# Sliding-window value products: a 64-column stationary side for the oldest key block

## The chip, the cores and the metric

The kernel runs on one core of a Trainium2 chip. The metric is device time in microseconds of one execution, the median of three runs. A core has TensorE (PE; its weight loads are listed as PEld), VectorE (DVE), ScalarE (ACT), GpSimd (POOL) and SyncE (SP), which here issues most DMAs. A matmul holds its stationary side (the weights, up to 128 rows by 128 columns) in the array and streams the moving side through it; the number of stationary columns is the number of partitions that it writes in PSUM.

## The reference

The model has four layers on x of 1 x 2048 x 512 in bf16, A, B, A, B, each with a residual: `x = x + layer(layernorm(x))`. Both have 32 heads of 16. A is linear attention. B, the part that matters here, is causal attention in a window of 256 keys:

```python
scores = jnp.einsum("bhqd,bhkd->bhqk", q, k) * (Dh ** -0.5)
mask = (idx[:, None] - idx[None, :] >= 0) & (idx[:, None] - idx[None, :] < W)   # W = 256
p = _softmax(jnp.where(mask[None, None], scores, -1e9), axis=-1)
o = jnp.einsum("bhqk,bhkd->bhqd", p, v)
```

## The kernel before

The 2048 tokens are 16 tiles (j) of 128. A `Plan` records every operation with what it reads and writes; `place` (L92) then gives each its engine, its place in the order and its PSUM bank from a table stored in the file (L872), and `synchronise` (L135) works out the semaphore waits. `play` (L988) sends each engine its operations in that order. So the order on every engine is fixed, and one operation can hold many instructions.

Two heads are worked on together: their keys (64 of each head) are interleaved to the 128 partitions of a key block b, so a tile of 128 tokens has two key blocks, 2j and 2j + 1. Sixteen such pairs of heads are numbered r = 4f + gq. For a layer B:

- `b_scores` (L634 to 670): scores of key block b of tile j against the queries that see it, matmuls of 32 rows by 128 columns (L650), four side by side in the array; then the exponential on ScalarE into the buffer pb (L660), and the causal mask on VectorE (L668).
- `b_far` (L672 to 725): the far 64 queries of a key block (L690, and in the last layer L693, with 32 x 64 tiles), the exponential (L703) and the mask of the window's end (L713 for a part, L721 and L722).
- The probabilities of a block lie as 320 columns of a row of 704: 384(b mod 2) + 0 to 320, and the 64 columns from 320 to 384 between the two blocks are zero. They are cleared once at the start (L364, "c24") and for a fourth buffer at L818 ("zero").
- `b_values` (L727 to 757): for each tile j, half h and f, one operation of 4 x (number of blocks) matmuls (L742). Each takes 128 columns of probabilities of one block as the stationary side and 34 columns of the values vB (2 heads x 16, and a column of ones for each head, for the sum) as the moving side, and adds to 34 columns of a PSUM bank. With j >= 2 a tile has six blocks, at the column offsets c = 0, -64, 64, 128, 192 and 256. At c = -64 the first 64 columns read are the zero pad, and at c = 256 the last 64 are. VectorE divides by the sums (L753, L754).
- `b_out` (L759): the transpose of the output, the product with wo (L412) and the residual (L585).

`feat` (L417 to 429) has 128-column matmuls for queries and keys (L426), `tok` (L404 to 415) 512-column ones (L412). The denominators of layer A (L554) use tiles of 128 rows by 32 columns. Layer B's work of a tile is interleaved with the projections of later tiles and the next layer's keys.

Of the kernel before, what the change touches and what calls it, by code (L numbers as in the profile page):

```python
# [11 lines left out]
P = 128  # L12
# [179 lines left out]
def dve(n, kind="psum"):  # L192

    if kind == "psum":
        return 65 + 1.04 * n, 148 + 1.04 * n
    if kind == "2x":
        return 68 + 0.52 * n, 151 + 0.52 * n
    if kind == "ptr":
        return 60 + 0.52 * n, 145 + 0.52 * n
    if kind == "4x":  # L200
        return 68 + 0.26 * n, 151 + 0.26 * n
    if kind == "recip":
        return 65 + 6.4 * n, 148 + 6.4 * n
    if kind == "bf":
        return 65 + 0.52 * n, 148 + 0.52 * n
    raise KeyError(kind)
# [23 lines left out]
class Plan:  # L230
# [496 lines left out]
    def b_values(self, j, h, key):  # L727
        K = self
        rp = self.rp
        ps = Tile(1, K.cls)  # L730
        blocks = [(2 * j, 0), (2 * j + 1, -64), (2 * j - 1, 64), (2 * j - 2, 128), (2 * j - 3, 192), (2 * j - 4, 256)]
        blocks = [(b, c) for b, c in blocks if b >= 0]
        reads = []
        for f in (2 * h, 2 * h + 1):
            def put(e, f=f):
                m = None
                for gq in range(4):
                    r = 4 * f + gq
                    u = 4 * (f - 2 * h) + gq
                    for i, (b, c) in enumerate(blocks):  # L740
                        o = 384 * (b % 2) + c
                        m = e.matmul(K.ps(ps)[:, 34 * u:34 * u + 34], K.P((b // 2) % rp)[:, f, gq % 2 * 2 + gq // 2, o:o + P], K.vB[:, (b // 2) % 4, b % 2, r, :], start=i == 0, stop=i == len(blocks) - 1)  # L742
                return m
            rd = []
            for i in range(max(0, j - 2), j + 1):
                rd += [("P", i % K.rp, f)] + [("vB", i % 4, a, b) for a in range(2) for b in range(2)]
                rd += [("P", i % K.rp, f, b, h_) for h_ in range(3) for b in (0, 1)]
            if j >= 2:
                rd += [("F", (j - 2) % K.rp, h_) for h_ in (0, 1)] + [("F", (j - 2) % K.rp, h_, 1) for h_ in (0, 1)]
            self.pe("pv", put, key - 0.001 * (f % 2), 4 * len(blocks), 34, rd=rd, ps=[ps])  # L750
        s = j % 2
        v = lambda: K.ps(ps)[:, 0:272].rearrange("p (u a d) -> p u a d", u=8, a=2)
        self.on("DVE", "rcp", lambda e: e.reciprocal(K.rc[:, s, h, :].rearrange("p (u a) -> p u a", a=2), v()[:, :, :, 16]), key + 0.02, dve(16, "recip"), wr=[("rc", s, h)], ps=[ps])  # L753
        self.on("DVE", "div", lambda e: e.tensor_tensor(  # L754
            K.o[:, s, :].rearrange("p (a r d) -> p r a d", a=2, d=DH)[:, 8 * h:8 * h + 8],
            v()[:, :, :, 0:16], K.rc[:, s, h, :].rearrange("p (u a) -> p u a", a=2).unsqueeze(3).to_broadcast([P, 8, 2, DH]), ALU.mult),
            key + 0.03, dve(256), rd=[("rc", s, h)], wr=[("o", s, h)], ps=[ps])
# [327 lines left out]
```

## Time and profile before

| | |
|---|---|
| median of 3 runs | 411.4 us (410.81 to 411.58) |
| the profiled execution | 410.39 us |
| its span | 408.7 us |
| granted TensorE clock | 1.00 |
| instructions | 18140, of which 7997 matmuls and as many weight loads in the page's count |

In the rows below a matmul group reads "line, engine, operation, output<-inputs, rows*columns of the stationary side, output shape, count | busy us, mean ns of one | idle time before it and what ended it". In the timeline the first two columns are start and length of a row of like instructions, in us from the start of the span. A matmul's length includes its way through the array, so like matmuls overlap, and their rate is read from their starts. In the rows of one line the three numbers are min, median and max of one instruction's length in ns.

### The profile page before, as it was taken

The numbers are of one execution on the slowest core, as the hardware profiler recorded it, in microseconds if no ns is written. First come the engines' busy times: TensorE is split into PE (matmuls) and PEld (weight loads), VectorE is DVE, ScalarE is ACT, GpSimd is POOL, SyncE is SP. The second block draws the span as 40 slices with busy tenths as digits, with TensorE's granted clock in tenths as the row PEclk, the third lists the DMA queues.
The fourth block names the chain that finished last, engine by engine and source line by source line (L and its number), as shares of the span: only waits on it lengthen the run. The fifth ranks groups of instructions, "written<-read, shape, count | busy, mean of one in ns | idle before, by whom it ended". The sixth has DMA issues, their size and how long they took to land.

```text
span 408.7 us, 18140 instructions
## 1 busy us (share of the span) xinstructions
PE 396.5 (97%) x7997; PEld 262.5 (64%) x7997; DVE 343.9 (84%) x819; ACT 355.7 (87%) x466; POOL 115.7 (28%) x185
## 2 busy tenths in 40 slices
PE   8999999999999999999999999999999999999996
PEld 3654776766575576565566777676756766566664
DVE  7985899899999898997778879988898867876675
ACT  2998769999999999999998265999999899999992
POOL 5746422113342231521322102111213123432132
PEclk9999999999999999999999999999999999999999
DMA  7794025833342443344143100345224542352463
GB/s 246 189 197 80 2 62 146 126 92 83 67 108 43 126 101 82 93 101 101 42 68 60 25 2 28 80 107 109 55 76 103 133 69 60 104 120 79 102 135 105
DMA packets 67750, 37.88 MB, mean 93 GB/s; under 512 B 48248, under 2 KB 62840, under 8 KB 67672
## 3 DMA queue, kind: packets, MB, share of 16 engines
q1 hardware_dynamic: 67328, 35.80, 38.1%
q8 instruction: 63, 1.03, 1.1%
q0 software_dynamic: 336, 0.92, 0.6%
q14 instruction: 15, 0.12, 0.1%
q10 hardware_dynamic: 8, 0.00, 0.0%
HBM read 6.29 MB, written 2.10 MB: 21 GB/s over the span
## 4 chain that ended last, share of the span: by engine, by line
PE 66%; ACT 22%; DVE 7%; DMA 2%; issue 1%; POOL 0%; SPq 0%
PE ps L412 23%; PE ps L426 16%; ACT pb L660 14%; PE ps L742 11%; PE ps L650 6%; PE ps L492 3%; ACT pb L703 3%; ACT vp L660 2%; DMA xT<-xn 2%; PE ps L693 2%; ACT tE L435 1%; PE ps L690 1%; ACT vp L703 1%; PE ps L468 1%; DVE XQ L574 1%
## 5 line engine op out<-in xcount | busy, mean ns | idle before, releaser
L660 ACT ACTIVATE pb<-ps 128x1024 bf16<-128x1024 f32 (+3 forms) x224 | 197.8, 977 | 8.3 <-PE ps L650 7.3
L742 PEld LDWEIGHTS ps<-vB,pb 128*128 128x128 bf16 x2560 | 77.9, 96 | 11.3 <-issue 3.6
L742 PE MATMUL ps<-vB,pb 128*128 128x34 bf16 x2560 | 83.7, 177 | 0.8 <-issue 0.5
L426 PE MATMUL ps<-xT,wBp 128*128 128x128 bf16 x1024 | 70.2, 219 | 0.6 <-DMA xT<-xn 0.6
L426 PEld LDWEIGHTS ps<-xT,wBp 128*128 128x128 bf16 x1024 | 58.6, 98 | 12.3 <-issue 4.2
L721 POOL TENSOR_SCALAR_AFFINE_SELECT pb<-pb 128x1024 bf16<-128x1024 bf16 x35 | 40.7, 1162 | 67.9 <-DVE pb L713 28.8
L375 POOL TENSOR_SCALAR ve<-mv 128x1 f32<-128x1 f32 x38 | 9.7, 254 | 158.3 <-DVE mv L374 157.7
L435 ACT ACTIVATE tE<-ps 128x512 bf16<-128x512 f32 x64 | 38.1, 608 | 16.6 <-PE ps L412 9.1
L703 ACT ACTIVATE pb<-ps 128x1024 bf16<-128x1024 f32 x50 | 49.2, 1053 | 2.3 <-PE ps L693 1.3
L650 PE MATMUL ps<-XQ,kB 32*128 32x256 bf16 (+2 forms) x1024 | 48.0, 262 | 2.6 <-DVE vp L603 0.6
L412 PE MATMUL ps<-wA,XQ 128*128 128x512 bf16 x192 | 49.4, 379 | 0.2 <-DVE XQ L574 0.2
L585 DVE TENSOR_TENSOR xres<-ps,xres 128x512 bf16<-128x512 f32 x63 | 42.9, 683 | 7.9 <-PE ps L412 7.6
L376 POOL TENSOR_TENSOR rs<-ve,negh 128x1 f32<-128x1 f32 x64 | 38.6, 604 | 36.1 <-DVE ve L375 31.7
L373 DVE BATCH_NORM_STATS2 stats<-xres 128x6 f32<-128x512 bf16 x64 | 43.6, 683 | 2.4 <-DMA xres<-in_A_x_dram 1.7
L426 PE MATMUL ps<-XQ,wA 128*128 128x128 bf16 x512 | 35.1, 219 | 0.1
L412 PE MATMUL ps<-wBv,xT 128*128 128x512 bf16 x128 | 35.0, 381 | 0.0
L650 PEld LDWEIGHTS ps<-XQ,kB 32*128 32x128 bf16 x1024 | 15.3, 92 | 30.7 <-ACT pb L660 9.5
L426 PEld LDWEIGHTS ps<-XQ,wA 128*128 128x128 bf16 x512 | 30.4, 98 | 5.7 <-issue 0.6
L412 PE MATMUL ps<-M,XQ 128*128 128x512 bf16 x128 | 33.7, 380 | 0.1
L412 PE MATMUL ps<-wBo,oT 128*128 128x512 bf16 x124 | 33.2, 381 | 0.3 <-ACT pb L660 0.3
L668 DVE TENSOR_TENSOR pb<-pb,tri 128x512 bf16<-128x512 bf16 x68 | 28.1, 417 | 3.8 <-ACT pb L660 3.4
L412 PEld LDWEIGHTS ps<-wA,XQ 128*128 128x128 bf16 x192 | 16.6, 97 | 18.1 <-issue 1.0
(120 smaller groups left out, 566.8 us busy)
## 6 DMA issues: line engine op xcount, KB each, us to landing
vB<-vS SPq DMA_DIRECT2D x64, 136.0 KB, 2.6
kB<-vp SPq DMA_DIRECT2D x64, 128.0 KB, 2.2
wA<-in_A_wqkv_dram SPq DMA_DIRECT2D x3, 512.0 KB, 5.2
xres<-in_A_x_dram SPq DMA_DIRECT2D x2, 512.0 KB
pb<-in_B_wqkv_dram SPq DMA_DIRECT2D x1, 1024.0 KB, 5.5
out_dram<-xres SPq DMA_DIRECT2D x8, 128.0 KB, 3.2
out_dram<-xres POOLq DMA_DIRECT2D x7, 128.0 KB, 2.8
xres<-in_A_x_dram SPq DMA_DIRECT2D x3, 256.0 KB, 3.2
```

The costliest lines, as they stand in the source:

```text
L373: self.on("DVE", "stats", lambda e: e.bn_stats(K.stats[:, t, :], K.xres[:, t, :]), key, dve(512), rd=[("xres", t)], wr=[("stats", t)])
L376: self.pow = self.on("POOL", "pow", lambda e: e.tensor_tensor(K.rs[:, t, :], K.ve[:, t, :], K.negh[:], ALU.pow), key + 0.03, (640, 690), r ...
L412: m = e.matmul(K.ps(ps), lhs(c), rhs(c), start=c == 0, stop=c == 3)
L426: m = e.matmul(K.ps(ps)[:, f * P:(f + 1) * P], w(c, f), xT(c), start=c == 0, stop=c == 3)
L435: self.on("ACT", "E", lambda e: e.activation(K.tE[:, s, :], K.ps(ps), ACT.Exp, bias=0.0), key, act(512), wr=[("tE", s)], ps=[ps])
L585: self.on("DVE", "res", lambda e: e.tensor_tensor(K.xres[:, t, :], K.ps(po), K.xres[:, t, :], ALU.add), key, dve(512), rd=[("xres", t)], w ...
L650: m = e.matmul(K.ps(two(gq // 2)[gq % 2])[:, ns * i:ns * i + ns], K.kB[rows, j % 4, 2 * f + b, :, :], K.XQ[rows, f, q:q + ns], start=True, ...
L660: return e.activation(out(h, ns).rearrange("p (f g) c -> p f g c", f=n), i, ACT.Exp, bias=0.0, scale=0.25)
L668: return e.tensor_tensor(x, x, K.tri[:, 0, :].unsqueeze(1).to_broadcast([P, 4 * n, 64]), ALU.mult)
L703: return e.activation(o.rearrange("p (f g) b c -> p f g b c", g=2), i, ACT.Exp, bias=0.0, scale=0.25)
L721: return e.affine_select(out=x, in_=x, compare_op=ALU.is_ge, fill=0.0, base=-2, pattern=[[0, 16], [-2, 64]], channel_multiplier=1)
L742: m = e.matmul(K.ps(ps)[:, 34 * u:34 * u + 34], K.P((b // 2) % rp)[:, f, gq % 2 * 2 + gq // 2, o:o + P], K.vB[:, (b // 2) % 4, b % 2, r, : ...
```

## The change

For tiles with j >= 2, the last two of the six blocks change places, so that the oldest block (2j - 4, at c = 256) is fifth and the one at c = 192 is last and closes the sum. The matmul of the oldest block takes 64 columns of probabilities, and writes 64 partitions, in place of 128: the 64 columns that are left out are the zero pad. Memory, masks, waits and the table of orders are as they were.

```diff
         blocks = [(b, c) for b, c in blocks if b >= 0]
+        if j >= 2:
+            blocks[-2:] = blocks[:-3:-1]
...
                         o = 384 * (b % 2) + c
-                        m = e.matmul(K.ps(ps)[:, 34 * u:34 * u + 34], K.P((b // 2) % rp)[:, f, gq % 2 * 2 + gq // 2, o:o + P], K.vB[:, (b // 2) % 4, b % 2, r, :], start=i == 0, stop=i == len(blocks) - 1)
+                        w = 64 if c == 256 else P
+                        m = e.matmul(K.ps(ps)[0:w, 34 * u:34 * u + 34], K.P((b // 2) % rp)[:, f, gq % 2 * 2 + gq // 2, o:o + w], K.vB[:, (b // 2) % 4, b % 2, r, :], start=i == 0, stop=i == len(blocks) - 1)
```

## The prediction

> **What bounds the kernel now.** I read the page first: busy time, the slices with the granted clock, then the costliest groups. After that come the busy times of the two stretches that hold all value products, and last the timeline of TensorE alone, because a busy PE in this profile is a modelled figure and has to be checked against start times.
>
> ```profile
> PE 396.5 (97%) x7997; PEld 262.5 (64%) x7997; DVE 343.9 (84%) x819; ACT 355.7 (87%) x466; POOL 115.7 (28%) x185
> ...
> PE   8999999999999999999999999999999999999996
> ...
> PEclk9999999999999999999999999999999999999999
> ...
> PE 66%; ACT 22%; DVE 7%; DMA 2%; issue 1%; POOL 0%; SPq 0%
> ...
> L742 PE MATMUL ps<-vB,pb 128*128 128x34 bf16 x2560 | 83.7, 177 | 0.8 <-issue 0.5
> ```
> ```profile
> sum 282.00, PE 272.06 PEld 182.09 DVE 235.12 ACT 264.53 POOL 75.19; mean PE 136.03 PEld 91.05 DVE 117.56 ACT 132.27 POOL 37.60
> ```
>
> The second fence is the sum over 76 to 220 us and 270 to 408 us. TensorE is idle there for 282.00 - 272.06 = 9.9 us and ScalarE for 282.00 - 264.53 = 17.5 us. The two are nearly balanced, with TensorE the fuller one and its clock never cut. The chain of waits gives 22% to ScalarE, but while the chain runs through ScalarE, TensorE has other work queued; what ScalarE really costs TensorE is inside those 9.9 us.
>
> The timeline around one value group of 48 products (start, length):
>
> ```profile
> 149.69 0.38 PE L412 MATMUL ps<-M,XQ 128*128 128x512 bf16 x1
> ...
> 150.00 0.40 PE L650 MATMUL ps<-XQ,kB 32*128 32x256 bf16 x8
> ...
> 150.33 1.37 PE L742 MATMUL ps<-vB,pb 128*128 128x34 bf16 x48
> ...
> 151.63 0.40 PE L650 MATMUL ps<-XQ,kB 32*128 32x256 bf16 x8
> ...
> 151.96 1.04 PE L412 MATMUL ps<-wBv,xT 128*128 128x512 bf16 x4
> ```
>
> A length runs to the end of the last matmul of the row. One product has a mean of 177 ns, so the 48 starts cover 1.37 - 0.177 = 1.19 us, 47 steps of 25 ns. The next row starts as soon as the previous ones let it: TensorE is issuing all the time. So whatever is added to the value products is added to the kernel, less what of the 9.9 us idle can be filled.
>
> **What the change does to the instruction stream.** In the built program 448 of the 2,880 value products (14 query tiles with j >= 2, 16 groups each, 2 layers) have a tile of 128 rows by 64 columns. All others keep 128x128. Each narrow product is fifth of six, so it has wide ones on both sides, inside its own group and in the next. No instruction goes away: the memsets of the zero pad stay (the block at c = -64 still reads the pad), as do the masks, the copies, the DMAs and every wait. On the four other engines the order is unchanged, and nothing moves past a queue. So the whole effect is this: 448 products with another shape, and 896 changes of TensorE's tile shape, two per narrow product.
>
> **Cost of a change of shape.** The trace has no 128x64 matmul, so I take the nearest rows, the denominators, which change only the columns (128x128 to 128x32 and back):
>
> ```profile
> 240.32 0.61 PE L426 MATMUL ps<-XQ,wA 128*128 128x128 bf16 x8
> 240.85 0.24 PE L554 MATMUL ps<-ones,eps 128*32 128x128 bf16 x4
> 240.92 0.40 PE L554 MATMUL ps<-XQ,zs 128*32 128x128 bf16 x16
> 241.25 0.62 PE L426 MATMUL ps<-XQ,wA 128*128 128x128 bf16 x8
> ```
> ```profile
> L426 PE MATMUL ps<-XQ,wA 128*128 128x128 bf16 x512 | 35.1, 219 | 0.1
> L554 PE MATMUL ps<-XQ,zs 128*32 128x128 bf16 x128 | 3.2, 219 | 0.0
> ```
>
> The last of the 8 wide ones starts at 240.32 + 0.61 - 0.219 = 240.71 us, the first 128x32 one at 240.85: 0.14 us instead of the usual step of (0.61 - 0.219)/7 = 56 ns. Back again: last start 240.92 + 0.40 - 0.219 = 241.10, next 241.25: 0.15 us. Each direction costs about 0.09 us above the step. The change of rows in the fence before gives the same: the last of 48 starts at 150.33 + 1.37 - 0.177 = 151.52, the next shape at 151.63, 0.11 us for a step that is 25 ns otherwise. I take 108 ns from a wide product to a narrow one, 83 more than 25.
>
> **Cost of the narrow load.** Two views show how long a matmul waits for its own weights, by its duration (min/median/max):
>
> ```profile
> L693 PE MATMUL ps<-XQ,kB x896: 184/209/213, 260.3 to 384.5; 32*64 32x64 bf16 x180
> ```
> ```profile
> L690 PE MATMUL ps<-XQ,kB x448: 188/188/198, 85.5 to 217.0; 32*128 32x64 bf16 x150
> ```
> ```profile
> L742 PE MATMUL ps<-vB,pb x2560: 177/177/191, 74.5 to 402.9; 128*128 128x34 bf16 x197
> ```
>
> L693 and L690 both move 64 columns; with a 64-column weight side a matmul lasts 209 ns, with 128 columns 188: 21 ns of waiting. The 191 of the third row belongs to the first product after a change of shape:
>
> ```profile
> 150.33 0.19 PE L742 MATMUL ps<-vB,pb 128*128 128x34 bf16 x1
> ```
>
> It lasts 191 - 177 = 14 ns longer, so the step to the second product is 25 + 14 = 39 ns. After a narrow product the way back is the moving time of 34 columns (56 ns for 128, so 14), the change (0.15 us - 0.056 = 94) and the wait for its weights (21): 129 ns.
>
> [...]
>
> **The sum.** Six starts of a group today: 6 x 25 = 150 ns. Afterwards: 39 + 3 x 25 + 108 + 129 = 351 ns. That is 201 ns per narrow product and 448 x 201 = 90.0 us on TensorE. Of this the idle time takes some: ScalarE and VectorE get that much more time for unchanged work, so most waits of TensorE for them shrink. I take 7 of the 9.9 us (the tiles j = 0 and 1 and the tail have waits that stay) and no new wait: TensorE's order is fixed, and ScalarE, for which score tiles are queued, only gets later input. 90.0 - 7 = 83 us. The profiled execution took 410.39 us (span 408.7 and 1.7 around it), giving 493.4; the median of the runs is 411.4, 1.0 above it, so **494.4 us**.
>
> Bounds: from below, both changes at 83 and no waits for loads, 448 x 166 = 74.4 us, with all 9.9 us filled: +64.5, 476 us. From above, the narrow load costs twice the 21 ns seen (128 rows are loaded, the row has 32): 222 x 448 = 99.5 us, nothing filled, and 3 us of new waits: +102.5, 514 us.
>
> **Rivals.**
> - *Only one of the two changes drains the array* (say narrow to wide is free, since the narrow tile is a corner of the wide array). Then a group costs about 150 + 83 + 14, 448 x 97 = 43.5 us less 7: 448 us. Against it: both directions of the denominators' rows cost the same.
> - *ScalarE sets the pace and hides part.* Its busy share in the stretches is 94%. If the 9.9 us of idle time were not the limit and half of the 90 us went behind it, the time is 456 us. Against it: the timeline shows TensorE without gaps, and ScalarE's idle 17.5 us would have to be time that TensorE could use.
> - *No drain at all*, because a 128x64 tile at the origin is no new shape to the array. Then the price is the load alone, 0 to 21 ns: up to +9.4 us, 411 to 421 us. No row excludes it, since no row has 128x64. [...]
> - *Faster.* No drain, and the 25 ns step is set by the weight load, so that half the columns take half the step: 12.5 x 448 = 5.6 us off, 406 us. It decides only if the cost of a change is under 6 ns, half the saving, against 94 in the rows. [...]
> - *The change does not do what it says*: it does, the shapes stand in the built program.
>
> **How the numbers follow.** Forecast (both changes drain, little hidden) 0.85; one drain 0.04; hidden behind ScalarE 0.03; no drain 0.06, of which a third each for slower, within 0.2% and faster; faster by a shorter load 0.02. The range is 474 to 514 us: the bounds of the forecast's case, which holds over 8 in 10 alone. A measurement tells about 0.2% from no change. Slower by over 0.2%: 0.85 + 0.04 + 0.03 + 0.02 = 0.94; within 0.02; faster 0.02 + 0.02 = 0.04.
>
> **What would show it.** A value group of 48 should last about 8 x 0.351 + 0.14 = 2.95 us instead of 1.37, the narrow ones standing alone between wide ones with about 0.11 and 0.13 us to their neighbours. ScalarE's share should fall to 355.7 / 492 = 72% and VectorE's to 70%, their busy times unchanged; TensorE's waits for ScalarE should shrink. The forecast is wrong if the narrow products start 25 ns after their neighbours (no drain), if only one side shows a gap, or if the groups grow as said and the span does not (then ScalarE, by a wait of TensorE for it, has the rest).

## The result, and the profile after

The changed kernel takes 547.27 us (543.86 to 549.96, four runs) against 411.16 us: 1.3305 times the time before, 95% interval 1.3225 to 1.3386. The forecast was 494.4 us, and its range ended at 514. The direction and the first mechanism were right; 53 us were missing from the sum.

The page of the changed kernel, the lines that answer to those of before (busy times, slices, clock, the chain that ended last, the value products' loads and products):

```profile
span 542.1 us, 18066 instructions
PE 523.5 (97%) x7923; PEld 350.3 (65%) x7997; DVE 343.3 (63%) x819; ACT 360.9 (67%) x466; POOL 114.9 (21%) x185
...
PE   8999999999999999999999999999999999999997
...
PEclk9999999997889879997899999987679866767566
...
PE 87%; DVE 5%; ACT 4%; issue 2%; DVEq 0%
...
L660 ACT ACTIVATE pb<-ps 128x1024 bf16<-128x1024 f32 (+3 forms) x224 | 200.6, 959 | 100.6 <-PE ps L650 100.4
L745 PE MATMUL ps<-vB,pb 128*128 128x34 bf16 (+1 forms) x2560 | 177.5, 188 | 0.3 <-DVE XQ L401 0.2
```

TensorE is the only bound left: the chain went from 66% to 87% TensorE, and ScalarE, with about the same work (360.9 us busy, before 355.7), now sits idle 100 us waiting for scores. The surprise is the line PEclk. It was 9 in all 40 slices; now it is under 9 in 20 of them, and the mean granted clock is 0.865.

The price of a change of tile shape is there as forecast ("drain" below: the stretch in which no product starts while the shape changes). One value group, weight loads of TensorE in four short windows that follow each other (start, length):

```profile
166.26 0.17 PEld L745 LDWEIGHTS ps<-vB,pb 128*128 128x128 bf16 x4
```
```profile
166.46 0.11 PEld L745 LDWEIGHTS ps<-vB,pb 128*64 128x64 bf16 x1
```
```profile
166.60 0.19 PEld L745 LDWEIGHTS ps<-vB,pb 128*128 128x128 bf16 x5
```
```profile
166.82 0.11 PEld L745 LDWEIGHTS ps<-vB,pb 128*64 128x64 bf16 x1
```

Loads that follow each other every 25 ns stop for the narrow one, which stands alone, and start again after it. From one narrow load to the next, 166.82 - 166.46 = 0.36 us, where six products took 150 ns. Products in a later stretch at full clock, where the rows of four begin with the narrow one and the rows of two are the wide pair before the next (start, length):

```profile
498.63 0.38 PE L745 MATMUL ps<-vB,pb 128*64 128x34 bf16 x4
498.85 0.20 PE L745 MATMUL ps<-vB,vp 128*128 128x34 bf16 x2
498.98 0.38 PE L745 MATMUL ps<-vB,pb 128*64 128x34 bf16 x4
499.21 0.20 PE L745 MATMUL ps<-vB,vp 128*128 128x34 bf16 x2
499.34 0.38 PE L745 MATMUL ps<-vB,pb 128*64 128x34 bf16 x4
```

The narrow one stands 0.13 us after the first of that pair, so 0.11 after the second. The next pair starts 0.22 to 0.23 us after the narrow one, and the steps of the three wide ones between take 39 + 25 + 25 ns of it, which leaves 0.13 to 0.14 for the way back. Read start by start, the two changes are 107 and 136 ns. A whole group of 48 at full clock takes 3.02 us (forecast 2.95, before 1.37):

```profile
166.27 3.02 PE L745 MATMUL ps<-vB,pb 128*128 128x34 bf16 x48
```

And this is how the clock goes. Busy times of the changed kernel in four windows of 3.41 us (PE, PEld, DVE, ACT, POOL, then the granted clock), and the timeline of TensorE there:

```profile
143.37:146.78 3.41, 3.41 (x15) 0.97 (x14) 2.02 (x5) 2.41 (x3) 0.00 (x0) 0.50 0.19 38
146.78:150.19 3.41, 3.41 (x64) 2.56 (x56) 1.88 (x6) 1.94 (x2) 0.00 (x0) 1.00 0.38 94
150.19:153.60 3.41, 3.08 (x31) 1.45 (x28) 2.39 (x7) 2.85 (x3) 0.00 (x0) 0.50 0.50 108
153.60:157.02 3.41, 3.41 (x86) 2.97 (x83) 1.36 (x5) 1.87 (x3) 0.79 (x2) 1.00 0.02 5
```
```profile
143.74 1.91 PE L412 MATMUL ps<-wA,XQ 128*128 128x512 bf16 x4
...
146.91 3.03 PE L745 MATMUL ps<-vB,pb 128*128 128x34 bf16 x48
149.87 0.40 PE L650 MATMUL ps<-XQ,kB 32*128 32x256 bf16 x8
150.60 1.49 PE L412 MATMUL ps<-wBo,oT 128*128 128x512 bf16 x3 [0.33 <-issue]
```

The clock is either whole or half, for one window or several. The window that begins at 146.78 holds a value group of 48 and little else; the next one, from 150.19, runs at half clock. In such a window TensorE has work, its products are only slow: three 512-column ones at 150.60 last 1.49 us and four at 143.74, in the half-clock window before, 1.91 us, both 0.44 us apart, where they are 0.22 apart at full clock. (The 0.33 us before 150.60 belong to a fourth one, whose record is missing; its weight load is there.) In this trace the clock has no other values than 0.50 and 1.00, and from one change of it to the next it is 3.41 us or a multiple of that (the longest stretch between two changes, at 1.00, lasts 88.75 us, 26 times 3.413).

What decides can be counted from the records. For each such window I added up the columns that its matmuls moved. A matmul in a 32-row strip counts as a quarter: four of 256 columns last 0.29 us in the trace of before, where one lasts 0.28 (L650). One on a 128 x 32 tile too: the 16 of 128 columns at 240.92 us there last 0.40 us together and one 0.22, so their starts lie within 0.18 us, where 16 steps of 56 ns would be 0.90. One on a 32 x 64 tile counts as an eighth, by its share of the area of a 128 x 128 one, which is my estimate; the trace of before shows 64 of 64 columns in 0.70 us, 8 ns from start to start (L693, at 260.33 us). The narrow products count whole. In these profiles 74 to 76 matmul records are missing, all of 512-column products, and they are counted by their weight loads, which are there. At full clock the 512-column products start every 216 ns and the 128-column ones every 56, so 384 columns take 160 ns, 2.4 a nanosecond, and a window has room for 8,192. The window from 146.78 has 48 x 34 = 1,632 and one group of scores, 8 x 256 / 4 = 512: 2,144, or 26%. Over the six profiles in which the clock changes often enough to find the windows (this one, and those of five experiments below):

| columns moved in the window | full-clock windows | followed by half clock | half-clock windows | followed by full clock |
|---|---|---|---|---|
| under 2,800 | 37 | 37 | 36 | 0 |
| 2,800 to 3,200 | 28 | 11 | 17 | 6 |
| over 3,200 | 687 | 0 | 41 | 41 |

The limit lies near 3,000 columns per window in both directions. That is 37% of what the array can move at full clock, but 73% at half clock, so a window that has once been lost is hard to win back: the low clock keeps itself low.

### The profile page after: what moved, and what is told of

It reads as the page before. It is cut to its first block, busy times and chain, and to the rows that moved or that the text cites. A ratio compares the mean times of both kernels' runs of the same rounds, so it can differ in the third digit from the quotient of the medians.

```text
span 542.1 us, 18066 instructions
## 1 busy us (share of the span) xinstructions
PE 523.5 (97%) x7923; PEld 350.3 (65%) x7997; DVE 343.3 (63%) x819; ACT 360.9 (67%) x466; POOL 114.9 (21%) x185
## 4 chain that ended last, share of the span: by engine, by line
PE 87%; DVE 5%; ACT 4%; issue 2%; DVEq 0%
PE ps L745 33%; PE ps L412 23%; PE ps L426 15%; PE ps L650 7%; PE ps L492 3%; ACT pb L660 2%; PE ps L693 2%; PE ps L1001 1%; PE ps L468 1%; DVE XQ L574 1%; PE ps L690 1%; ACT tE L435 1%; DVE xres L585 1%; ACT pb L703 1%; PE ps L274 1%
## 5 line engine op out<-in xcount | busy, mean ns | idle before, releaser
L660 ACT ACTIVATE pb<-ps 128x1024 bf16<-128x1024 f32 (+3 forms) x224 | 200.6, 959 | 100.6 <-PE ps L650 100.4
L745 PE MATMUL ps<-vB,pb 128*128 128x34 bf16 (+1 forms) x2560 | 177.5, 188 | 0.3 <-DVE XQ L401 0.2
L745 PEld LDWEIGHTS ps<-vB,pb 128*128 128x128 bf16 (+1 forms) x2560 | 140.6, 101 | 38.4 <-issue 5.8
L756 DVE RECIPROCAL rc<-ps 128x16 f32<-128x16 f32 x64 | 16.4, 257 | 106.8 <-PE ps L745 106.6
L426 PE MATMUL ps<-xT,wBp 128*128 128x128 bf16 x1024 | 79.8, 236 | 0.0
L426 PEld LDWEIGHTS ps<-xT,wBp 128*128 128x128 bf16 x1024 | 67.3, 106 | 12.8 <-issue 6.2
L650 PE MATMUL ps<-XQ,kB 32*128 32x256 bf16 (+2 forms) x1024 | 53.9, 290 | 1.5 <-ACT vp L703 0.5
L412 PE MATMUL ps<-wA,XQ 128*128 128x512 bf16 x176 | 50.7, 410 | 2.3 <-issue 0.9
L376 POOL TENSOR_TENSOR rs<-ve,negh 128x1 f32<-128x1 f32 x64 | 38.1, 596 | 45.7 <-DVE ve L375 41.6
L745 PE MATMUL ps<-vB,vp 128*128 128x34 bf16 (+1 forms) x320 | 41.5, 196 | 0.0
L412 PE MATMUL ps<-wBo,oT 128*128 128x512 bf16 x104 | 35.7, 453 | 3.4 <-issue 2.0
L650 PEld LDWEIGHTS ps<-XQ,kB 32*128 32x128 bf16 x1024 | 15.8, 95 | 35.5 <-ACT pb L660 10.1
```

The lines of the kernel that those rows point to most:

```text
L376: self.pow = self.on("POOL", "pow", lambda e: e.tensor_tensor(K.rs[:, t, :], K.ve[:, t, :], K.negh[:], ALU.pow), key + 0.03, (640, 690), r ...
L412: m = e.matmul(K.ps(ps), lhs(c), rhs(c), start=c == 0, stop=c == 3)
L426: m = e.matmul(K.ps(ps)[:, f * P:(f + 1) * P], w(c, f), xT(c), start=c == 0, stop=c == 3)
L650: m = e.matmul(K.ps(two(gq // 2)[gq % 2])[:, ns * i:ns * i + ns], K.kB[rows, j % 4, 2 * f + b, :, :], K.XQ[rows, f, q:q + ns], start=True, ...
L660: return e.activation(out(h, ns).rearrange("p (f g) c -> p f g c", f=n), i, ACT.Exp, bias=0.0, scale=0.25)
L745: m = e.matmul(K.ps(ps)[0:w, 34 * u:34 * u + 34], K.P((b // 2) % rp)[:, f, gq % 2 * 2 + gq // 2, o:o + w], K.vB[:, (b // 2) % 4, b % 2, r, ...
```

## The experiments

**Theory:** two prices. Each change of TensorE's tile shape drains the array (wide to narrow 107 ns from start to start, back 136, and 39 to the second wide product in place of 25 each), and the value products then move so few columns per microsecond that the clock is halved. **Rivals:** the price is on any stationary side under 128 columns; the price is on each narrow product; the shape changes themselves halve the clock.

**The order alone.** Blocks exchanged, all products 128 wide:

```diff
-                        w = 64 if c == 256 else P
+                        w = P
```

> Only the exchange of the last two blocks, all products 128 columns wide. Both theories: 411 us, a value group of 48 in 1.37 us, clock 1.00. If the order had a price of its own, it would show here.

Measured: 412.62 us, ratio 1.0012 (0.9978 to 1.0047), span 408.8 us. The exchange of the blocks costs nothing that can be measured.

**72 columns.** The same with 72 columns, narrower than 128 but wider than 64:

```diff
-                        w = 64 if c == 256 else P
+                        w = 72 if c == 256 else P
```

> The oldest block has 72 columns in place of 64, so the tile stays 128x128 and no shape changes. Theory (the change of tile shape costs, 208 ns per narrow product at full clock in the trace of the changed kernel): no drain, only a slower load of 0 to 35 ns for 448 products, 411 to 427 us, clock 1.00. Rival (any stationary side under 128 columns costs the gap): about 25 + 200 ns per product and the clock falls as in the changed kernel, 540 us.

Measured: 414.9 us, ratio 1.0046 (1.0021 to 1.0071), span 413.1 us, clock 0.999. Its line PEclk, and the groups of the value products by shape (busy, mean ns of one):

```profile
PEclk9999999999999999999999999999999999999999
...
L745 PE MATMUL ps<-vB,pb 128*128 128x34 bf16 x2160 | 88.2, 177 | 0.9 <-issue 0.6 <-DVE XQ L401 0.2
L745 PEld LDWEIGHTS ps<-vB,pb 128*128 128x128 bf16 x2160 | 82.0, 97 | 11.3 <-issue 4.1 <-ACT pb L660 2.0 <-DVE pb L668 0.8
L745 PE MATMUL ps<-vB,pb 128*72 128x34 bf16 x400 | 65.8, 187 | 0.4 <-issue 0.4
L745 PEld LDWEIGHTS ps<-vB,pb 128*72 128x72 bf16 x400 | 44.0, 110 | 0.5 <-issue 0.5
```

A 72-column load lasts 110 ns, one of 128 columns 97, and its product takes 10 ns longer (187 against 177). 448 x 10 = 4.5 us, of which the time shows 1.6 (414.9 less 413.35, the kernel before on the same chip). So eight columns more leave 2 us of the 136 that the changed kernel lost. A group of 48 takes 1.45 us (before 1.37, the changed kernel 3.02), so a side under 128 columns is not what costs: 64 columns have the two gaps, 72 have none. That the array takes 64 columns as another tile shape and 72 as the whole one is my reading of this; the rows give sizes alone. Fewer columns are no saving either, the narrower load is the slower one. (The 35 ns that the expectation allows for a load was an estimate that no run shows; measured are 13 ns more in the load and 10 in the product.)

**Side by side.** In an operation, 20 wide products first, then its four narrow ones:

```diff
-                    for i, (b, c) in enumerate(blocks):
+                todo = [(gq, i) for gq in range(4) for i in range(len(blocks)) if blocks[i][1] != 256]
+                todo += [(gq, i) for gq in range(4) for i in range(len(blocks)) if blocks[i][1] == 256]
+                for n, (gq, i) in enumerate(todo):
...
```

(The marks for the start and the stop of a sum then stand at the first and the last product of the operation.)

> The four 64-column products of an operation stand side by side behind its 20 wide ones: 224 shape changes in place of 896, the same 448 narrow products. Theory (price per change): an operation costs 14 + 82 + 112 = about 208 ns for its two changes and up to 35 ns for each narrow load, 112 operations, 23 to 39 us more on TensorE, 425 to 450 us, clock near 1.00. Rival (price per narrow product): as the changed kernel, 540 us.

Measured: 429.73 us, ratio 1.0396 (1.035 to 1.0442), span 427.7 us, clock 0.996. All 448 narrow products are there, with a quarter of the changes, and 19.0 us of the 133.4 by which the span had grown are left. Priced per change it is 112 x 208 ns = 23 us, with 4 hidden (or 7, by the 16.4 us between the medians, 429.73 and the 413.35 of the kernel before on the same chip). The price is on the change, not on the narrow product:

```profile
L747 PE MATMUL ps<-vB,pb 128*64 128x34 bf16 x400 | 30.0, 189 | 0.0
```

against 84.7 us busy for the same 400 in the changed kernel:

```profile
L745 PE MATMUL ps<-vB,pb 128*64 128x34 bf16 x400 | 84.7, 212 | 0.0
```

**One moving column.** The kernel before, with as much time added but no shape change:

```diff
+                        for _ in range(8 if i == 4 and len(blocks) == 6 else 0):
+                            e.matmul(K.ps(ps)[:, 300:301], K.P((b // 2) % rp)[:, f, gq % 2 * 2 + gq // 2, o:o + P], K.vB[:, (b // 2) % 4, b % 2, r, 0:1], start=False, stop=False, skip_group_check=True)
```

> The kernel before, all products 128 wide in the old order, with 8 more 128-column products of one moving column for each group of six (they write PSUM columns that nobody reads): 8 x 25 = 200 ns more per group, about what the two shape changes add, and no shape change; 448 groups, 90 us on TensorE. In a group 6 x 34 + 8 columns move in 350 ns, as little as in the changed kernel. Theory (the clock is halved in windows in which little moves through the array): the clock falls to 0.85 to 0.90 and the time is 530 to 550 us. Rival (the shape changes, or the gaps without a matmul that they make, halve the clock): the clock stays 1.00 and the time is 490 to 500 us.

Measured: 540.3 us (four runs, 535.52 to 546.94), ratio 1.3041 (1.2957 to 1.3126). The profile is that of the longest, span 545.2 us, clock 0.871; the other three have 0.871 to 0.886. Its page:

```profile
PE 520.4 (95%) x11505; PEld 373.9 (69%) x11581; DVE 344.2 (63%) x819; ACT 361.5 (66%) x466; POOL 114.9 (21%) x185
...
PEclk9999999997868878997899999979687769877676
```

Nearly the same line PEclk as that of the changed kernel, with no shape change added and products every 25 ns. So neither the drain nor a gap is needed to lose the clock (0.871 here, 0.865 in the changed kernel): few columns moving through the array are enough.

**A quarter and a half of the narrow products:**

```diff
-                        w = 64 if c == 256 else P
+                        w = 64 if c == 256 and gq < 1 else P      # and gq < 2
```

> Narrow products for one of the four gq of an operation: 112 narrow ones, 224 shape changes, one per operation of 24. Price per change: 112 x 208 ns = 23 us, less what is hidden, 425 to 434 us, about the same as with four narrow ones side by side, which has the same number of changes. Activity theory: a value group of 48 moves 48 x 34 columns in 1.6 us, the rest of a clock window of 3.4 us is dense, so the clock stays over 0.98. Rival (each change throttles): a quarter of the loss of the changed kernel, clock about 0.965, 435 to 450 us.

Measured: 432.56 us, ratio 1.0488 (1.043 to 1.0546), span 431.6 us, clock 0.991.

> Narrow products for two of the four gq: 224 narrow ones, 448 shape changes. Changes: 224 x 208 ns = 47 us, less some 8 hidden. Activity theory: a value group of 48 takes 2.2 us; a window of 3.4 us with one group in it stands near half activity, so the clock falls in part of the windows, less than proportionally: 0.95 to 0.99, 450 to 470 us. Rival (each change throttles): half of the loss, clock 0.93, 475 to 480 us.

Measured: 462.6 us, ratio 1.1207 (1.1141 to 1.1272), span 457.7 us, clock 0.977. Spans over that of before (408.7): 112 narrow products 22.9 us, 224 49.0, 448 133.4. The first two are 204 and 219 ns each, near the price of the two changes; the last is 298. The loss is not proportional, as a limit on the clock would have it. (By the medians, each against that of the kernel before that was run beside it, the three are 19.9, 49.9 and 136.1 us, or 177, 223 and 304 ns each.) The quarter also has as many changes as the version side by side, with a quarter of the narrow products, and costs about as much (22.9 against 19.0 us): again the change is what counts.

**Fillers.** The changed kernel, with one or three wide products of 238 moving columns more in each group of six:

```diff
+                        for _ in range(1 if i == 1 and len(blocks) == 6 else 0):      # and range(3 ...)
+                            e.matmul(K.ps(ps)[:, 272:510].rearrange("p (u d) -> p u d", d=34), K.P((b // 2) % rp)[:, f, gq % 2 * 2 + gq // 2, o:o + P], K.vB[:, (b // 2) % 4, b % 2, 0:7, :], start=False, stop=False, skip_group_check=True)
```

> The changed kernel, and in each group of six one more 128-column product with 238 moving columns (into PSUM columns that nobody reads), 102 ns each, 46 us for 448. In a group 6 x 34 + 238 = 442 columns move in 460 ns, 40% of the array's cycles against 24%. Activity theory with the limit near half: the clock is still cut but less, 0.88 to 0.95, 560 to 590 us. Rival (each change throttles): 896 changes as before, the same lost time as in the changed kernel, 547 + 46 = 593 us at a clock of 0.87.

Measured: 551.18 us, ratio 1.3361 (1.3284 to 1.3438), span 546.5 us, clock 0.994. This is outside both expectations, and on the theory's side: 46 us of work more than in the changed kernel, and 4 us more time. The clock came back almost whole at 40% of the columns, so the limit that I had put near half is lower; the table above has it at 37%.

```profile
PE 527.5 (97%) x8371; PEld 372.7 (68%) x8445; DVE 344.0 (63%) x819; ACT 360.1 (66%) x466; POOL 114.7 (21%) x185
...
PEclk9999999999999999999999999999998999899999
```

> The changed kernel, and in each group of six three such products, 137 us for 448. 918 columns move in 664 ns, 58% of the array's cycles, as much as in the value groups before the change (34 columns in 25 ns, 57%). Activity theory: the clock is back at 1.00 in spite of the 896 shape changes, and the time is 411 + 93 (the changes) + 137 less some 8 hidden, 625 to 640 us. Rival (each change throttles): the clock loss stays, 547 + 137 = 684 us at 0.89.

Measured: 637.03 us, ratio 1.5451 (1.5365 to 1.5537), span 635.4 us, clock 1.000, with all 896 changes. Its line PEclk, and from the timeline the bare price of a group (the three fillers, then the products to the next ones):

```profile
PEclk9999999999999999999999999999999999999999
...
189.94 0.46 PE L747 MATMUL ps<-vB,pb 128*128 128x238 bf16 x3
190.24 0.51 PE L745 MATMUL ps<-vB,pb 128*128 128x34 bf16 x6
190.60 0.47 PE L747 MATMUL ps<-vB,pb 128*128 128x238 bf16 x3
190.91 0.51 PE L745 MATMUL ps<-vB,pb 128*128 128x34 bf16 x6
191.27 0.47 PE L747 MATMUL ps<-vB,pb 128*128 128x238 bf16 x3
```

From filler to filler 0.66 to 0.67 us; less three times 102 ns (238 columns at 2.4 a nanosecond, and the 2.7 ns that the 512-column step of 216 ns has beyond its 213.3) leaves 0.357 us for six products, 207 ns more than 150. Spans: 448 x 207 ns = 92.7 us and 448 x 306 = 137.1 make 229.8; measured 635.4 - 408.7 = 226.7. By the medians on one chip the difference is 637.03 - 412.71 = 224.3. With one filler, 92.7 + 45.7 = 138.4; measured 137.8, in which the windows that its clock of 0.994 still lost are contained. So the sum closes to 3 to 6 us once the clock is whole.

## Why the prediction was wrong

- **What bounds the kernel: right.** It is TensorE, issuing without gaps. The added time went through, and ScalarE's share fell to 67%, where 72% was named for a shorter span.
- **The instruction stream, 448 products and 896 changes: right.** The exchange of the blocks costs nothing.
- **Cost of a change, from the columns-only rows of the denominators: right.** Forecast 108 ns in, 129 out, 39 to the next, 351 a group; measured 107, 136, 39 and 357. The way out is 7 ns longer. 90.0 us forecast, 92.7 measured. The one-drain and no-drain rivals and the faster one fall with it.
- **Cost of the narrow load: near.** It stood in the sum as 21 ns of waiting where a wide one has 14, 7 more. Measured are 7 ns more than forecast on the way out, and 7 per step where narrow ones follow each other (32 ns for 25).
- **Hidden time: not settled.** 7 us were taken off. The runs with a whole or nearly whole clock show 3 to 7 (three fillers 3 by the spans and 5.5 by the medians on one chip, side by side 4 and 7). The kernel before itself took 409.96 to 415.81 us in the runs beside the experiments, with clocks of 0.991 to 1.000, so 3 and 7 can't be told apart.
- **The sum: the step that failed.** It multiplied steps measured at clock 1.00 and never asked whether the clock would stay there. "Its clock never cut" was read as a property of the kernel; it was a result of how many columns the value groups move, 34 in 25 ns, 57% of the array, and the change took that to 204 columns in 357 ns, 24%, for 3 us at a time, nearly a whole window. Without it the span would be 408.7 + 92.7 less 3 to 7, about 494 to 498 us and a time of 496 to 500, inside the range. With it the span is 542.1: 44 to 48 us are the clock. The mean clock of 0.865 means 0.135 x 542.1 / 0.5 = 146 us at half clock. That they cost some 46 and not 73 fits with what stretches there: the steps of the 512-column products double (0.44 us for 0.22), but drains and loads stretch little. From 501.8 to 518.8 us, at half clock, the loads of the value products last 104 to 109 ns for 128 columns and 128 for 64; from 495.0 to 501.7, at full clock, 96 and 106. In a stretch at half clock the narrow products (the rows that begin with one) stand 0.42 us apart, where they are 0.36 apart at full clock:

```profile
506.87 0.38 PE L745 MATMUL ps<-vB,vp 128*64 128x34 bf16 x2
507.08 0.28 PE L745 MATMUL ps<-vB,pb 128*128 128x34 bf16 x4
507.29 0.38 PE L745 MATMUL ps<-vB,vp 128*64 128x34 bf16 x2
507.50 0.28 PE L745 MATMUL ps<-vB,pb 128*128 128x34 bf16 x4
507.71 0.38 PE L745 MATMUL ps<-vB,vp 128*64 128x34 bf16 x2
```

- **Rivals:** five were named, none of them a lower clock. A rival of the form "so few columns move that the clock is cut" could have been named from before's own rows, by the columns per microsecond that the forecast itself implied. The limit could not be read there, since the clock of before is whole in all of its slices.

What stays open: the exact limit (between 2,800 and 3,200 columns the windows go both ways), and what within the array the clock follows. It is not the loads: 128 columns loaded for one moving column did not keep the clock up (0.871).

## What to carry to other kernels

Before a stationary side is made narrower, time one such product among wide ones and look for a gap on both sides of it (64 columns had them here, 72 had not): a lone product of another shape cost two drains here, 207 ns, as much as eight of its wide neighbours; put such products side by side, or leave the pad in. And a sum over TensorE has two factors: after adding up the steps, divide the columns moved by the time of each stretch of 3.4 us; where that falls under 3,000 columns, the limit found here (37% of the array's rate), count the dense work beside it at half clock.

## What the runs showed of the hardware that was not expected

- TensorE's clock halved while TensorE was busy 97% of the time and had few waits: it follows the columns moved per window (limit near 3,000 in 3.41 us), not how busy the engine looks. 3,584 products with one moving column each, 90 us at full clock, cost about 126 us (539.62, the median of the three shorter runs, less 413.35, the kernel before on the same chip).
- The same limit on the way back makes the low clock sticky: it is 37% of the full rate and 73% of the half rate.
- Useless work can be nearly free: 448 fillers of 102 ns, 46 us, lengthened the span by 4.4 us (542.1 to 546.5), because they brought the clock from 0.865 to 0.994.
- A stationary side of 72 columns loads in 110 ns and one of 128 in 97: narrower was slower even where no gap was left (414.9 us, and 413.35 before).
